# Top-k attention with two expert layers: the mask moves to ScalarE, copies out of PSUM to VectorE

## The chip, the cores and the metric

One core of a Trainium2 chip runs the whole program. The metric is the device time of one execution in microseconds; the time of a kernel is the median over its runs. The engines are TensorE (PE in the profile; PEld are its weight loads), VectorE (DVE), ScalarE (ACT), GpSimd (POOL) and SyncE (SP), which issues most of the loads. Each engine works through its own queue in program order and waits on semaphores of the others.

## The reference, cut to what matters

```python
# q, k, v: (2 batches, 8 heads, 576 tokens, 64)
scores = q @ k.T / 8
kth    = 32nd largest score of each row
scores = where(scores >= kth, scores, -1e9) - max(row)
attn   = exp(scores) / (sum(exp(scores)) + 1e-9)
x      = attn @ v                        # laid out as (1152 tokens, 512)
p      = domain_probs / (sum + 1e-9)     # (1152, 4)
x      = sum over 4 experts e of p[:, e] * (relu(x @ w1[e]) @ w2[e])   # hidden 1024
h      = max(x @ m1, x @ m2, x @ m3)     # hidden 768
out    = h @ w_out
```

Only the softmax's numerator and the ReLU outputs are touched by the change. The four last weights arrive as 64-bit floats and are turned into 32-bit floats in the kernel.

## The kernel before

The 1152 tokens are 9 tiles of 128. Four chunks of 2, 2, 2 and 3 tiles are worked on in turn, and a *pair* is one tile with two heads: 36 pairs, 8 for each of the first three chunks and 12 for the last. The tile in the middle holds tokens of both batches. A pair computes two score rows of 576 per token (`scores`, L349), copies them out of PSUM on ScalarE (L357), finds the 32 largest in seven steps of VectorE (`topk`: four MAX8, L370, and three MATCH_REPLACE8, L372), takes the exponential on ScalarE against the row's maximum (`exp`, L383), and puts those below the 32nd to zero (`mask`). The mask is one operation of VectorE with the row sum beside it (L390) for 57 of the 72 heads; for pairs 0 to 7 (second head: 0 to 6) it is two operations of GpSimd (L393, L394) and a summing copy on ScalarE (L398). Then TensorE transposes p (L408, L413), ScalarE copies the transposes out of PSUM (L411, L416), TensorE multiplies with v (L451, L454), and VectorE multiplies with the reciprocal of the sum, which went through TensorE too (L436, L438, L461).

Attention is laid out in *slots*: pair n begins at slot 8n, its second head `stag` slots later, and each step has an offset in the dictionaries `FIRST` (pairs 0 to 6), `TIGHT` (pair 7) and `LOOSE` (the rest). In a slot with `scores`, `trans`, `pv` the TensorE work is queued; what takes it out of PSUM is queued `lag` slots later.

All matmuls with weights are done as three products of high and low parts of both operands (L588 to L590), in fp32r. The weights come by SyncE's queue in tiles of 128x1024, ScalarE makes the high part (L225), GpSimd the low part (L229), from the fourth phase on VectorE every second one. A hidden activation is made in the same way: ScalarE writes the ReLU as high part (L666) and VectorE the low part from PSUM (L668); every fourth (`ON_POOL_H = 4`) is copied out first (L659) and split by ScalarE and GpSimd (L660, L661).

The products run as a generator of eight phases: the experts of chunks 0 to 3, then the last two layers of chunks 0 to 3. A planner interleaves it with the slots: `dve(n)` and `pe(n)` add planned times of VectorE (0.07 + n/960 us) and TensorE (n/2400 us), and after each slot the products go on until TensorE's planned time has caught up with VectorE's, taken times `SHARE` of the phase. The experts of a chunk begin when its x is there (`x_ready`), with the products over all but the last head pair first (`begun`). From slot 306 on, behind attention, 48 pieces of the last four weights are converted (`to_float32`, L196 to L208), stored to DRAM (L213) and loaded again as weights.

Of the kernel before, what the change touches and what calls it, by code (L numbers as in the profile page):

```python
# [10 lines left out]
F32 = mybir.dt.float32  # L11
# [3 lines left out]
AF = mybir.ActivationFunctionType  # L15
ALU = mybir.AluOpType
PSUM = bass.MemoryType.PSUM

TOPK = 32

BEGIN, READY = 4, 4
SPLIT_K, SPLIT_Q = 8, 10
ON_POOL_H = 4
ON_POOL_E = (0, 1)
H_LAG, E_LAG = 0, 0
WAITING = 3
PAUSE = 0.8
LATE = 3
ON_POOL = ((0, 1, 2, 3, 4, 5, 6, 7), (0, 1, 2, 3, 4, 5, 6))
W_FIRST, W_AHEAD = 60, 4  # L30
WIDE, W_FROM, W_STEP = 4, 306, 2

FIRST = dict(stag=2, new=1, scores=-12, trans=11, pv=17, rec=16, lag=2, sum=4)
TIGHT = dict(stag=3, new=1, scores=-7, trans=9, pv=14, rec=12, lag=1, sum=0)
LOOSE = dict(stag=4, new=1, scores=-4, trans=9, pv=16, rec=14, lag=2, sum=0)

EARLY = 7

SHARE, AHEAD = (1.0, 0.95, 1.0, 1.0), 6
AHEAD_S = 5  # L40

PHASES = [(1, 0), (1, 1), (1, 2), (1, 3), (2, 0), (2, 1), (2, 2), (2, 3)]
# [8 lines left out]
def kernel(  # L51
# [14 lines left out]
    nc = tc.nc  # L66
    B, HP, D, _, S = k.shape
    NT, DM = out.shape
    E = gates.shape[2]
    P = 128  # L70
# [3 lines left out]
    NR = S // P  # L74
    TAIL = S - NR * P
    NTILE = NT // P
    SCALE = 1.0 / float(D) ** 0.5
# [13 lines left out]
    at = ctx.enter_context(tc.tile_pool(name="at", bufs=2))  # L91
# [17 lines left out]
    def dve(n):  # L109
        clock["dve"] += 0.07 + n / 960.0  # L110

    def pe(n):
        clock["pe"] += n / 2400.0

    def bank(name):
        return pg.tile([P, 512], F32, tag="g", name=name)
# [212 lines left out]

    class Pair:  # L330
        def __init__(self, n):
            self.c, self.hp, self.t = pairs[n]
            self.s, self.w, self.m, self.nb = {}, {}, {}, {}
            self.p = self.rs = None
            self.pt = {}

            self.did = set()

            self.on_pool = [n in ON_POOL[j] for j in range(2)]

        def scores(self, j):
            srcs = [(b, i) for i, (t, b) in enumerate(SLOTS[self.c]) if t == self.t]
# [30 lines left out]

        def negate(self, j):
            m = self.m[j]
            self.nb[j] = at.tile([P, 1], F32, tag="nb%d" % j, name="nb")
            nc.scalar.activation(out=self.nb[j], in_=m[:, 0:1], func=AF.Copy, scale=-SCALE)

        def exp(self, j):
            if self.p is None:  # L380
                self.p = at.tile([P, 2, S], F32, tag="p", name="p")
                self.rs = at.tile([P, 2], F32, tag="rs", bufs=3, name="rs")
            nc.scalar.activation(out=self.p[:, j].rearrange("p (a n) -> p a n", a=2), in_=self.s[j], func=AF.Exp, bias=self.nb[j], scale=SCALE)  # L383

        def mask(self, j):
            p = self.p[:, j].rearrange("p (a n) -> p a n", a=2)
            s, kth, total = self.s[j], self.m[j][:, TOPK - 1:TOPK], self.rs[:, j:j + 1]
            if not self.on_pool[j]:
                dve(S)
                nc.vector.scalar_tensor_tensor(out=p, in0=s, scalar=kth, in1=p, op0=ALU.is_ge, op1=ALU.mult, accum_out=total)  # L390
                self.did.update([("p", j), ("sum", j)])
                return lambda: None
            nc.gpsimd.tensor_scalar(out=s, in0=s, scalar1=kth, scalar2=None, op0=ALU.is_ge)  # L393
            nc.gpsimd.tensor_tensor(out=p, in0=p, in1=s, op=ALU.mult)  # L394
            self.did.add(("p", j))

            def add():
                nc.scalar.activation(out=s, in_=p, func=AF.Copy, accum_out=total)  # L398
                self.did.add(("sum", j))
            return add  # L400

        def trans_p(self, part):
            assert {("p", j) for j in range(2) if part in (j, 2)} <= self.did
            ps = bank("psp")
            pe(260 * (NR if part < 2 else 1))
            if part < 2:
                for r in range(NR):
                    nc.tensor.transpose(ps[:, r * P:(r + 1) * P], self.p[:, part, part * TAIL + r * P:part * TAIL + (r + 1) * P], ident)  # L408
                d = at.tile([P, NR, P], F32, tag="pt%d" % part, bufs=1, name="pt")
                self.pt[part] = d  # L410
                return lambda: [nc.scalar.activation(out=d, in_=ps.rearrange("p (r n) -> p r n", r=NR), func=AF.Copy),  # L411
                                self.did.add(("pt", part))]
            nc.tensor.transpose(ps[:, 0:P], self.p.rearrange("p j s -> p (j s)")[:, NR * P:NR * P + 2 * TAIL], ident)  # L413
            d = at.tile([P, P], F32, tag="pt2", name="pt4")
            self.pt[2] = d
            return lambda: [nc.scalar.activation(out=d, in_=ps[:, 0:P], func=AF.Copy), self.did.add(("pt", 2))]  # L416

        def guard(self):
            assert {("sum", 0), ("sum", 1)} <= self.did
# [56 lines left out]
    def attention():  # L476

        NP = len(pairs)
        prs = {}
        later = {}  # L480

        def options(n):
            return FIRST if n < EARLY else TIGHT if pairs[n][0] == 0 else LOOSE

        def at_slot(s, f, *a):
            later.setdefault(s, []).append((f, a))


        first_use = {}
        for n, (c, hp, t) in enumerate(pairs):  # L490
            for b in ((0, 1) if t == MIXED else (0 if t < MIXED else 1,)):
                first_use.setdefault(("k", b, hp), n)
            first_use.setdefault(("q", c, hp), n)
        free = {"k": -99, "q": -99}
        for key, n in first_use.items():
            s0 = 8 * n
            if n == 0:
                if key[0] == "k":
                    at_slot(-60, load_first)
                    at_slot(-50, split_first)  # L500
                    free["k"] = free["q"] = -50
                    at_slot(s0, load_v, *key[1:])
                continue
            load, split = (load_k, split_k) if key[0] == "k" else (load_q, split_q)
            at = max(s0 + options(n)["scores"] - (SPLIT_K if key[0] == "k" else SPLIT_Q), free[key[0]] + 2)
            at_slot(max(at - 15, free[key[0]] + 1), load, *key[1:])
            at_slot(at, split, *key[1:])
            free[key[0]] = at
            if key[0] == "k":
                at_slot(s0, load_v, *key[1:])  # L510
        for n, (c, hp, t) in enumerate(pairs):
            s0 = 8 * n
            prs[n] = Pair(n)
            pr = prs[n]
            o = options(n)

            def two(s, f, *a, lag=o["lag"]):
                at_slot(s, lambda: at_slot(s + lag, f(*a)))
            for j in range(2):
                b0 = s0 + o["stag"] * j  # L520
                two(b0 + o["scores"], pr.scores, j)
                for i in range(7):
                    if o["new"]:
                        later.setdefault(b0 + i, []).insert(0, (pr.topk, (j, i)))
                    else:
                        at_slot(b0 + i, pr.topk, j, i)
                at_slot(b0 + 2, pr.negate, j)
                at_slot(b0 + 5, pr.exp, j)
                two(b0 + 7, pr.mask, j, lag=o["sum"] if n < EARLY else 3)
                two(b0 + o["trans"], pr.trans_p, j)  # L530
            two(s0 + o["stag"] + o["trans"], pr.trans_p, 2)
            at_slot(s0 + o["rec"] - 1, pr.guard)
            at_slot(s0 + o["rec"], pr.recip)
            at_slot(s0 + o["rec"] + 1, pr.spread)
            at_slot(s0 + o["pv"], pr.pv)
            two(s0 + o["rec"] + 2, pr.trans_r)
            end = max(o["pv"], o["rec"] + 2) + o["lag"]
            at_slot(s0 + end + 1, pr.norm)
            two(s0 + end + 2, pr.split_x)
        last = {}  # L540
        for n, p in enumerate(pairs):
            o = options(n)
            last[p[0:2]] = 8 * n + max(o["pv"], o["rec"] + 2) + 2 * o["lag"] + 2
        end = max(last.values()) + 1
        s = min(later)
        while s <= end:
            todo = later.pop(s, [])
            i = 0
            while i < len(todo):
                f, a = todo[i]  # L550
                f(*a)
                todo += later.pop(s, [])
                i += 1
            yield s, [c for c in last if last[c] + (READY if c[1] == HP - 2 else 0) == s]
            s += 1

        while narrowed[0] < WIDE * len(wide):
            clock["dve"] += PAUSE
            yield s, []
            s += 1  # L560


    lag = []
# [351 lines left out]
```

## Time and profile before

| | |
|---|---|
| median of 3 runs | 806.25 us (805.86 to 808.3) |
| profiled execution | 808.2 us, its span 806.4 us |
| busy, share of the span | PE 93%, PEld 82%, DVE 85%, ACT 61%, POOL 65% |
| granted TensorE clock, mean | 0.943 |
| chain that ended last | DVE 41%, PE 35%, DMA 8%, issue 6% |

The busy shares are means over stages with different limits, so the table says little by itself: the same TensorE runs at half its clock in the first tenth of the span and at the full clock in most of the rest.

### The profile page before, as it was taken

The page shows a single profiled execution, that of the slowest core. Times are in us where ns is not written, and L with a number is a line of the kernel's source. Part 1 is how long each engine was busy: PE and PEld are TensorE (multiplying, and loading weights), DVE is VectorE, ACT ScalarE, POOL GpSimd, SP SyncE. Part 2 cuts the span into 40 slices and gives each one's busy share as a digit, 9 for nine tenths or more (in the row PEclk, how much of TensorE's full clock was granted, in tenths as well). Part 3 has the DMA queues.
Part 4 walks back from the last instruction along what each step waited for, and adds up shares of the span by engine and source line. Part 5 has one row for each costly group of instructions (what it writes and reads, how often), then busy time and mean ns, then how long its engine had stood idle before and what let it go on. Part 6 is the DMA issues. An engine that isn't in the chain of part 4 may idle for free.

```text
span 806.4 us, 13973 instructions
## 1 busy us (share of the span) xinstructions
PE 746.3 (93%) x4942; PEld 663.2 (82%) x4942; DVE 683.8 (85%) x1242; ACT 492.7 (61%) x1027; POOL 527.2 (65%) x316
## 2 busy tenths in 40 slices
PE   3776799999999989999999999989999898999998
PEld 2454699888898879888888987879988697989996
DVE  6999989999999999999999996999999683445441
ACT  5666768677776775766777665665565444545541
POOL 2787968779888876668777685566565473555330
PEclk8556599999999999999999999999999899999999
DMA  3430245636545445253534364877777455656531
GB/s 98 117 106 13 68 131 147 190 117 173 174 137 171 135 146 151 88 169 112 161 126 146 112 188 152 270 249 250 245 251 243 157 178 167 232 165 208 178 102 40
DMA packets 50214, 126.24 MB, mean 157 GB/s; under 512 B 7904, under 2 KB 18144, under 8 KB 50144
## 3 DMA queue, kind: packets, MB, share of 16 engines
q1 hardware_dynamic: 41936, 116.69, 46.8%
q10 hardware_dynamic: 8208, 8.65, 3.1%
q8 instruction: 39, 0.64, 0.3%
q14 instruction: 31, 0.25, 0.1%
HBM read 116.67 MB, written 8.65 MB: 155 GB/s over the span
## 4 chain that ended last, share of the span: by engine, by line
DVE 41%; PE 35%; DMA 8%; issue 6%; POOL 4%; ACT 4%; SPq 2%; ACTq 0%; DVEq 0%; POOLq 0%
DVE m L370 14%; DVE work L372 13%; PE ps L588 9%; PE ps L590 9%; PE ps L589 9%; DVE p L390 6%; DMA narrow<-narrow 3%; POOL wlo L229 2%; DMA raw<-in_w_dram 2%; DVE h L668 2%; ACT whi L225 2%; SPq L246 2%; DMA kraw<-in_k_dram 1%; PE pso L590 1%; PE pso L588 1%
## 5 line engine op out<-in xcount | busy, mean ns | idle before, releaser
L229 POOL TENSOR_TENSOR wlo<-raw,whi 128x1024 fp32r<-128x1024 f32 x136 | 336.5, 2487 | 162.6 <-ACT whi L225 155.8
L225 ACT ACTIVATE whi<-raw 128x1024 fp32r<-128x1024 f32 x176 | 182.9, 1058 | 73.7 <-DMA raw<-narrow 23.8
L588 PE MATMUL ps<-xl,whi 128*128 128x256 f32 (+1 forms) x512 | 155.3, 303 | 1.7 <-DVE h L668 0.8
L370 DVE MAX8 m<-work 128x8 f32<-128x576 f32 x216 | 154.6, 742 | 0.1
L589 PE MATMUL ps<-xh,whi 128*128 128x256 f32 (+1 forms) x512 | 152.6, 298 | 0.0
L590 PE MATMUL ps<-xh,wlo 128*128 128x256 f32 (+1 forms) x512 | 152.6, 298 | 0.0
L229 DVE TENSOR_TENSOR wlo<-raw,whi 128x1024 fp32r<-128x1024 f32 x40 | 61.6, 1541 | 66.4 <-ACT whi L225 64.9
L372 DVE MATCH_REPLACE8 work<-m,work 128x576 f32<-128x576 f32 x144 | 106.4, 740 | 0.0
L588 PEld LDWEIGHTS ps<-xl,whi 128*128 128x128 f32 x512 | 99.0, 193 | 3.7 <-DVE h L668 1.3
L589 PEld LDWEIGHTS ps<-xh,whi 128*128 128x128 f32 x512 | 98.8, 193 | 0.9
L590 PEld LDWEIGHTS ps<-xh,wlo 128*128 128x128 f32 x512 | 98.7, 193 | 0.0
L590 PE MATMUL ps<-x2h,wlo 128*128 128x256 f32 (+1 forms) x288 | 85.4, 296 | 0.8 <-DVE wlo L229 0.8
L588 PE MATMUL ps<-x2l,whi 128*128 128x256 f32 (+1 forms) x288 | 85.3, 296 | 0.0
L589 PE MATMUL ps<-x2h,whi 128*128 128x256 f32 (+1 forms) x288 | 85.2, 296 | 0.0
L390 DVE SCALAR_TENSOR_TENSOR p<-s,m,p 128x576 f32<-128x576 f32 x57 | 81.0, 1422 | 0.0
L588 PE MATMUL ps<-wlo,h 128*128 128x512 f32 x192 | 77.7, 405 | 0.0
L590 PE MATMUL ps<-whi,h 128*128 128x512 f32 x192 | 75.3, 392 | 0.0
L589 PE MATMUL ps<-whi,h 128*128 128x512 f32 x192 | 75.3, 392 | 0.0
L408 PE MATMUL psp<-ident,p 128*128 128x128 f32 x288 | 50.8, 306 | 26.3 <-POOL p L394 15.4
L208 POOL TENSOR_TENSOR narrow<-narrow,raw 128x256 int32<-128x256 int32 x48 | 41.2, 858 | 44.7 <-DVE narrow L205 14.6
L349 PE MATMUL pss<-kT,ql 128*128 128x288 f32 x160 | 55.1, 358 | 13.9 <-DVE ql L293 7.6
L408 PEld LDWEIGHTS psp<-ident,p 128*128 128x128 f32 x288 | 38.3, 156 | 32.9 <-POOL p L394 18.9
(104 smaller groups left out, 1706.0 us busy)
## 6 DMA issues: line engine op xcount, KB each, us to landing
raw<-in_w_dram SPq DMA_DIRECT2D x128, 512.0 KB, 3.9
raw<-narrow SPq DMA_DIRECT2D x48, 512.0 KB, 3.8
raw<-in_m_dram SPq DMA_DIRECT2D x36, 256.0 KB, 4.4
narrow<-narrow ACTq DMA_DIRECT2D x48, 128.0 KB, 3.7
kraw<-in_k_dram SPq DMA_DIRECT2D x14, 288.0 KB, 4.5
raw<-in_mo_dram SPq DMA_DIRECT2D x12, 256.0 KB, 4.2
vt<-in_v_dram SPq DMA_DIRECT2D x8, 288.0 KB, 4.2
out_dram<-ob ACTq DMA_DIRECT2D x9, 256.0 KB, 2.0
```

The lines of the kernel that those rows point to most:

```text
L208: nc.gpsimd.tensor_tensor(out=out.bitcast(I32), in0=out.bitcast(I32), in1=last, op=ALU.add)
L225: nc.scalar.activation(out=hi, in_=raw, func=AF.Copy)
L229: on.tensor_tensor(out=lo, in0=raw, in1=hi.bitcast(F32), op=ALU.subtract)
L246: nc.sync.dma_start(out=out[half * D:(half + 1) * D], in_=src)
L349: nc.tensor.matmul(ps[:, 0:SH], lhsT=l, rhs=r, start=i == 0, stop=i == len(mm) - 1)
L370: nc.vector.max(m[:, 8 * r:8 * r + 8], src)
L372: nc.vector.match_replace(out=self.w[j], in_to_replace=m[:, 8 * r:8 * r + 8], in_values=src, imm_value=NEG)
L390: nc.vector.scalar_tensor_tensor(out=p, in0=s, scalar=kth, in1=p, op0=ALU.is_ge, op1=ALU.mult, accum_out=total)
L408: nc.tensor.transpose(ps[:, r * P:(r + 1) * P], self.p[:, part, part * TAIL + r * P:part * TAIL + (r + 1) * P], ident)
L588: nc.tensor.matmul(ps, lhsT=lh, rhs=rl, start=first, stop=False)
L589: nc.tensor.matmul(ps, lhsT=lh, rhs=rh, start=False, stop=False)
L590: nc.tensor.matmul(ps, lhsT=ll, rhs=rh, start=False, stop=last)
```

## The change

The mask goes to ScalarE for all heads. A first pass writes `prelu(kth - s)` with the slope 2^-100 on the side of the kept scores, so that those below the 32nd are positive and the kept ones are tiny and not positive; a [128, 1] operation makes the bias `kth/8 - max/8`; a second pass takes the exponential with a scale of -2^100/8, which gives the kept scores their exponential and the others zero, and sums the row. It is queued at offset 7, where the mask was (the exponential was at 5). From pair 7 on VectorE copies the transposed p out of PSUM. All low parts of ReLU outputs are made by VectorE (`ON_POOL_H = 0`). `trans`, `pv` and `rec` move one slot later in `LOOSE` and one, two and three slots earlier in `FIRST`; `SHARE` is 1 in the second phase; v is queued 8 slots later (`LATE_V`).

```diff
--- before.py
+++ after.py
@@ -19,24 +19,23 @@
 TOPK = 32
 
 BEGIN, READY = 4, 4
-SPLIT_K, SPLIT_Q = 8, 10
-ON_POOL_H = 4
+SPLIT_K, SPLIT_Q, LATE_V = 8, 10, 8
+ON_POOL_H = 0
 ON_POOL_E = (0, 1)
 H_LAG, E_LAG = 0, 0
 WAITING = 3
 PAUSE = 0.8
 LATE = 3
-ON_POOL = ((0, 1, 2, 3, 4, 5, 6, 7), (0, 1, 2, 3, 4, 5, 6))
 W_FIRST, W_AHEAD = 60, 4
 WIDE, W_FROM, W_STEP = 4, 306, 2
 
-FIRST = dict(stag=2, new=1, scores=-12, trans=11, pv=17, rec=16, lag=2, sum=4)
-TIGHT = dict(stag=3, new=1, scores=-7, trans=9, pv=14, rec=12, lag=1, sum=0)
-LOOSE = dict(stag=4, new=1, scores=-4, trans=9, pv=16, rec=14, lag=2, sum=0)
-
+FIRST = dict(stag=2, new=1, scores=-12, trans=10, pv=15, rec=13, lag=2)
+TIGHT = dict(stag=3, new=1, scores=-7, trans=9, pv=14, rec=12, lag=1)
+LOOSE = dict(stag=4, new=1, scores=-4, trans=10, pv=17, rec=15, lag=2)
 EARLY = 7
-
-SHARE, AHEAD = (1.0, 0.95, 1.0, 1.0), 6
+SMALL = 2.0 ** -100
+
+SHARE, AHEAD = (1.0, 1.0, 1.0, 1.0), 6
 AHEAD_S = 5
 
 PHASES = [(1, 0), (1, 1), (1, 2), (1, 3), (2, 0), (2, 1), (2, 2), (2, 3)]
@@ -329,14 +328,13 @@
 
     class Pair:
         def __init__(self, n):
+            self.n = n
             self.c, self.hp, self.t = pairs[n]
             self.s, self.w, self.m, self.nb = {}, {}, {}, {}
             self.p = self.rs = None
             self.pt = {}
 
             self.did = set()
-
-            self.on_pool = [n in ON_POOL[j] for j in range(2)]
 
         def scores(self, j):
             srcs = [(b, i) for i, (t, b) in enumerate(SLOTS[self.c]) if t == self.t]
@@ -373,47 +371,47 @@
 
         def negate(self, j):
             m = self.m[j]
-            self.nb[j] = at.tile([P, 1], F32, tag="nb%d" % j, name="nb")
-            nc.scalar.activation(out=self.nb[j], in_=m[:, 0:1], func=AF.Copy, scale=-SCALE)
+            self.nb[j] = at.tile([P, 2], F32, tag="nb%d" % j, name="nb")
+            nc.scalar.activation(out=self.nb[j][:, 0:1], in_=m[:, 0:1], func=AF.Copy, scale=-SCALE)
 
         def exp(self, j):
+
+
+
             if self.p is None:
                 self.p = at.tile([P, 2, S], F32, tag="p", name="p")
                 self.rs = at.tile([P, 2], F32, tag="rs", bufs=3, name="rs")
-            nc.scalar.activation(out=self.p[:, j].rearrange("p (a n) -> p a n", a=2), in_=self.s[j], func=AF.Exp, bias=self.nb[j], scale=SCALE)
-
-        def mask(self, j):
             p = self.p[:, j].rearrange("p (a n) -> p a n", a=2)
-            s, kth, total = self.s[j], self.m[j][:, TOPK - 1:TOPK], self.rs[:, j:j + 1]
-            if not self.on_pool[j]:
-                dve(S)
-                nc.vector.scalar_tensor_tensor(out=p, in0=s, scalar=kth, in1=p, op0=ALU.is_ge, op1=ALU.mult, accum_out=total)
-                self.did.update([("p", j), ("sum", j)])
-                return lambda: None
-            nc.gpsimd.tensor_scalar(out=s, in0=s, scalar1=kth, scalar2=None, op0=ALU.is_ge)
-            nc.gpsimd.tensor_tensor(out=p, in0=p, in1=s, op=ALU.mult)
-            self.did.add(("p", j))
-
-            def add():
-                nc.scalar.activation(out=s, in_=p, func=AF.Copy, accum_out=total)
-                self.did.add(("sum", j))
-            return add
+            kth, nb = self.m[j][:, TOPK - 1:TOPK], self.nb[j]
+            nc.scalar.activation(out=p, in_=self.s[j], func=AF.Prelu, bias=kth, scale=-1.0, alpha=SMALL)
+            nc.scalar.activation(out=nb[:, 1:2], in_=kth, func=AF.Identity, bias=nb[:, 0:1], scale=SCALE)
+            nc.scalar.activation(out=p, in_=p, func=AF.Exp, bias=nb[:, 1:2], scale=-SCALE / SMALL, accum_out=self.rs[:, j:j + 1])
+            self.did.update([("p", j), ("sum", j)])
+
+        def copy(self, out, ps, n):
+
+            if self.n < EARLY:
+                nc.scalar.activation(out=out, in_=ps, func=AF.Copy)
+            else:
+                dve(n)
+                nc.vector.tensor_copy(out=out, in_=ps)
 
         def trans_p(self, part):
             assert {("p", j) for j in range(2) if part in (j, 2)} <= self.did
             ps = bank("psp")
+            copy = self.copy
             pe(260 * (NR if part < 2 else 1))
             if part < 2:
                 for r in range(NR):
                     nc.tensor.transpose(ps[:, r * P:(r + 1) * P], self.p[:, part, part * TAIL + r * P:part * TAIL + (r + 1) * P], ident)
                 d = at.tile([P, NR, P], F32, tag="pt%d" % part, bufs=1, name="pt")
                 self.pt[part] = d
-                return lambda: [nc.scalar.activation(out=d, in_=ps.rearrange("p (r n) -> p r n", r=NR), func=AF.Copy),
+                return lambda: [copy(d, ps.rearrange("p (r n) -> p r n", r=NR), NR * P),
                                 self.did.add(("pt", part))]
             nc.tensor.transpose(ps[:, 0:P], self.p.rearrange("p j s -> p (j s)")[:, NR * P:NR * P + 2 * TAIL], ident)
             d = at.tile([P, P], F32, tag="pt2", name="pt4")
             self.pt[2] = d
-            return lambda: [nc.scalar.activation(out=d, in_=ps[:, 0:P], func=AF.Copy), self.did.add(("pt", 2))]
+            return lambda: [copy(d, ps[:, 0:P], P), self.did.add(("pt", 2))]
 
         def guard(self):
             assert {("sum", 0), ("sum", 1)} <= self.did
@@ -507,7 +505,7 @@
             at_slot(at, split, *key[1:])
             free[key[0]] = at
             if key[0] == "k":
-                at_slot(s0, load_v, *key[1:])
+                at_slot(s0 + LATE_V, load_v, *key[1:])
         for n, (c, hp, t) in enumerate(pairs):
             s0 = 8 * n
             prs[n] = Pair(n)
@@ -525,8 +523,7 @@
                     else:
                         at_slot(b0 + i, pr.topk, j, i)
                 at_slot(b0 + 2, pr.negate, j)
-                at_slot(b0 + 5, pr.exp, j)
-                two(b0 + 7, pr.mask, j, lag=o["sum"] if n < EARLY else 3)
+                at_slot(b0 + 7, pr.exp, j)
                 two(b0 + o["trans"], pr.trans_p, j)
             two(s0 + o["stag"] + o["trans"], pr.trans_p, 2)
             at_slot(s0 + o["rec"] - 1, pr.guard)
```

## Rows read from the trace of the kernel before

**Rows 1.** Busy times by stage: stretch, us, each engine's busy us, granted clock, DMA share, GB/s.
```profile
0.00:97.50 97.50, 62.01 (x295) 46.44 (x296) 89.03 (x194) 62.64 (x170) 70.41 (x57) 0.63 0.26 75
...
120.00:480.00 360.00, 350.21 (x2651) 311.65 (x2651) 355.30 (x721) 254.15 (x552) 280.16 (x151) 0.99 0.49 146
480.00:499.40 19.40, 16.75 (x96) 12.88 (x93) 11.41 (x19) 9.50 (x22) 9.11 (x6) 0.91 0.44 137
499.40:660.00 160.60, 154.78 (x821) 139.88 (x820) 148.06 (x208) 91.38 (x172) 94.19 (x71) 0.98 0.73 235
660.00:806.40 146.40, 140.04 (x917) 131.64 (x915) 59.93 (x63) 60.77 (x78) 58.16 (x26) 1.00 0.47 155
```

**Rows 2.** TensorE in order of time: start, us, line, operation, count, idle before, releaser.
```profile
97.50 0.41 PE L588 MATMUL ps<-xl,whi 128*128 128x256 f32 x1
...
162.77 0.47 PE L408 MATMUL psp<-ident,p 128*128 128x128 f32 x1 [2.91 <-DVE h L668]
...
489.64 0.57 PE L588 MATMUL ps<-wlo,h 128*128 128x512 f32 x1
...
499.38 0.33 PE L588 MATMUL ps<-xl,whi 128*128 128x384 f32 x1
...
637.89 0.79 PE L588 MATMUL ps<-wlo,hh 128*128 128x512 f32 x1 [3.19 <-DVE acc L697]
...
674.78 0.50 PE L588 MATMUL pso<-wlo,h 128*128 128x512 f32 x1 [1.78 <-ACT h L794]
```

**Rows 3.** Groups by line and shape. Columns: operation, count, busy us, mean ns, idle before it.
```profile
L390 DVE SCALAR_TENSOR_TENSOR p<-s,m,p 128x576 f32<-128x576 f32 x57 | 81.0, 1422 | 0.0
...
L383 ACT ACTIVATE p<-s,nb 128x576 f32<-128x576 f32 x72 | 55.8, 774 | 0.0
...
L411 ACT ACTIVATE pt<-psp 128x512 f32<-128x512 f32 x72 | 42.7, 593 | 3.1 <-PE psp L408 3.0
...
L393 POOL TENSOR_SCALAR s<-s,m 128x576 f32<-128x576 f32 x15 | 25.9, 1724 | 11.1 <-DVE m L370 5.4 <-ACT pt L416 3.4 <-ACT s L357 2.0
L668 DVE SCALAR_TENSOR_TENSOR h<-ps,h 128x512 fp32r<-128x512 f32 x36 | 24.3, 675 | 5.9 <-ACT h L666 5.9
...
L394 POOL TENSOR_TENSOR p<-p,s 128x576 f32<-128x576 f32 x15 | 21.1, 1405 | 1.3
...
L377 ACT ACTIVATE nb<-m 128x1 f32<-128x1 f32 x72 | 14.1, 198 | 12.3 <-DVE m L370 12.3
...
L461 DVE TENSOR_TENSOR xt<-psv,r 128x128 f32<-128x128 f32 x36 | 10.0, 278 | 4.4 <-ACT r L438 4.4
...
L104 ACT ACT_TABLE_LOAD x1 | 1.3, 1283 | 0.7 <-PEq L894 0.7
```

**Rows 4.** Chain of waits in order of time. Columns: start, us, what.
```profile
147.59 1.25 POOL ql L293
...
154.69 5.68 DMA raw<-in_w_dram
160.45 1.06 ACT whi L225
...
664.45 1.85 DMA narrow<-narrow
```

**Rows 5.** VectorE in order of time, two pairs' reciprocals.
```profile
81.22 0.15 DVE L427 RECIPROCAL rr<-rs 128x2 f32<-128x2 f32 x1
...
90.58 0.15 DVE L427 RECIPROCAL rr<-rs 128x2 f32<-128x2 f32 x1
```

**Rows 6.** The conversions' tile, first and last start.
```profile
L196 ACT ACTIVATE narrow<-raw x48: 412/428/453, 490.9 to 650.6; 128x256 f32<-128x256 f32 x48
```

**Rows 7.** ScalarE's waits from 120 to 480 us. Columns: total us, times, longest.
```profile
ACT nb L377 <- DVE m L370: 12.3, 12, 2.6
ACT whi L225 <- DMA raw<-in_w_dram: 12.2, 9, 4.4
...
ACT r L438 <- PE psr L436: 9.5, 11, 1.4
```

## The prediction

> **What bounds the kernel now.** I read the busy times by stage first, then TensorE's order of time at its gaps, then the chain of waits, and last the groups of instructions for prices. The stages are cut where the work changes [rows 1]. From 0 to 97.5 us only attention runs: VectorE is busy 89.0 us of 97.5, TensorE 62.0 at a granted clock of 0.63. From 97.5 to 499.4 attention and the products of the first three chunks of tokens share the chip, and TensorE and VectorE are both full: in 120 to 480 us TensorE is busy 350.2 of 360 and VectorE 355.3. From 499.4 to 660 the experts of the last chunk run while 48 pieces of weights are converted: TensorE 154.8 of 160.6, VectorE 148.1. After 660 TensorE is nearly alone, 140.0 of 146.4.
>
> So the change, which mostly unloads VectorE, has to be read from TensorE. A VectorE that has room lets the end move only by what TensorE now stands still: 9.8 us in 120 to 480, 2.7 in 480 to 499.4, 5.8 in 499.4 to 660, 6.4 after that (of which the last store is a part), and by what the lower clock costs after such stops, 0.01 of 360, 0.09 of 19.4 and 0.02 of 160.6 us: 3.6, 1.7 and 3.2 [rows 1]. That is 33 us at most. The matmuls between the gaps follow each other closely (42 of 512 columns between 489.64 and 499.38, 0.232 us each, [rows 2]) and stay as they are.
>
> **The change, part by part.** Durations are of the profiled execution: span 806.4, 808.2 with what lies around it; the median of the runs is 806.25, so I work out a difference and take it from the median.
>
> *Masks.* VectorE loses 57 masks of 1.422 us, 81.0 us [rows 3]. GpSimd loses 15 of 1.724 and 1.405, 47 us, all of it before 97.5 [rows 3]. ScalarE gains 72 first passes; the trace has none of that function, and the nearest row is its own exponential over the same tile, 0.774 us [rows 3]. Between the 0.593 of a 512-column copy below and twice the exponential above, I take 0.774; with a [128,1] operation of 0.198 [rows 3] and as much for reading the sum, 1.17 us a head, 84 us in all.
>
> *Copies out of PSUM.* 29 pairs give VectorE two copies of 512 columns and one of 128. It has none in the trace; the nearest rows read one PSUM operand too: 0.675 for 512 columns, 0.278 for 128 [rows 3]. From 0.593 (ScalarE's own copy) to 0.74 (a MAX8 of 576 columns is about that) for the large one; I take 0.675: 29 x (2 x 0.675 + 0.278) = 47.2 us. ScalarE loses about 29 x (2 x 0.593 + 0.278) = 42.5. The copy waits for TensorE's transposes; behind it on VectorE stand the MAX8 of later heads. It is queued two slots after the transposes (one for pair 7) and VectorE has room, so I price the wait at nothing; without that room each copy could hold VectorE one slot.
>
> *Low parts of ReLU outputs.* Every fourth goes from GpSimd to VectorE: 12 of 0.675 before 499.4 and 4 of two halves after it, 8.1 and at most 5.4 us. VectorE ends at 81.0 - 47.2 - 8.1 = 26 us less up to 499.4, which is 7% of that stage, and some 5 more after it. ScalarE is 254 us busy of 360 [rows 1]; its balance there is 28 pairs x (2 x 1.17 - 1.46), less 12 second copies of ReLU outputs at about the 0.6 of a 512-column copy: +17, to 271, 75%. Both have room; TensorE has not. VectorE's saving by itself is therefore worth only TensorE's gaps.
>
> *Gaps in 120 to 480.* The longest is 2.91 us at 162.77 [rows 2]. Its chain begins on GpSimd: a low part of q at 147.59 frees the buffer that SyncE's queue waits for, the weights behind it land at 160.4, ScalarE's high part follows, and the ReLU, its low part and a mask stand behind that [rows 4]. GpSimd loses 47 us of masks ahead of this place and 12 low parts along the stage, and v is queued 8 slots later, so weights come earlier. The transposes of later chunks also stand one slot later behind their mask. Against it: the exponential now stands on ScalarE behind the same weights. Of 9.8 + 3.6 us I let two thirds go: -8.8, between 0 and -13.4.
>
> *Earlier start.* In the first pairs x is ready 3 slots earlier (2 x lag + 2 behind 15 instead of 18). A pair's reciprocals are 9.36 us apart there, so a slot is 1.17 us [rows 5], and the first products, now at 97.5 [rows 2], come 3.5 us earlier: -3.5, between 0 and -3.5.
>
> *Order of TensorE.* The planner issues products against VectorE's planned time. 12 more low parts at 0.603, 29 x 1.409 for copies instead of 57 x 0.67 for masks, and the share 0.95 that becomes 1 over about a third of 360 us: 7.2 + 2.7 + 6 = 16 us more, beside the earlier start. Today 9.7 us of the third chunk's products are left when attention's last transposes are issued (489.64 to 499.38, [rows 2]). They will be spent before, and the last pair's way from mask to x has nothing under it: TensorE stands about 7 us there, clock included, instead of 2.7 + 1.7: +2.6, between 0 and +6. The last chunk's experts then start at 499.4 - 3.5 - 8.8 + 2.6 = 489.7.
>
> *The tail.* Gaps of 5.8 + 3.2 us up to 660 are mostly accumulations late on VectorE (3.19 us at 637.89, [rows 2]). GpSimd's wide low parts go, VectorE gets 5 us more: I let half of it go, -4.6, between +3 and -9. But the conversions still begin behind attention. Today the last one is stored from 664.45 and TensorE waits 1.78 us for its weights at 674.78 [rows 2, 4]. TensorE, 10 us earlier at its experts and without the 9.7 us left over, comes to that place with less under the last conversion: the 10.3 us from that store to the product, less some 3 by which ScalarE leads TensorE there today (an estimate from the planner's counts), are 7.5 us of wait instead of 1.8: +5.7, and a clock that falls after it, +1.7 as at 480 to 499.4. Between 0 and +12.
>
> Sum: -3.5 - 8.8 + 2.6 - 4.6 + 5.7 + 1.7 = -6.9; 806.25 - 6.9 = 799.4 us.
>
> **Rivals.**
> 1. *The gaps close wholly.* With 1 us left in attention, 5 at its end and 4 at the last conversion, the span is 94.0 + (401.9 - 17.8) + 6 = 484 at the experts of the last chunk, then 299 to 303: 783 to 787. For it: VectorE gets 7% of room. Against it: the gap with the longest chain is no gap of VectorE's own.
> 2. *The conversions hold the tail.* They begin about 1 us ahead of the experts, at 488.6, and last as long as today, from 490.9 [rows 6] to 664.4, 173.5 us, with VectorE 92% busy under them, or 4.4 longer with the new low parts: 662 to 666.5 plus the 142 that follow, 804 to 808.5, no change to speak of. Against it: TensorE's gaps under them are 5.8 us in all, so over most of the stage the pieces follow its pace and don't set it.
> 3. *ScalarE becomes the bound, slower.* The exponential now waits for the 32nd value, the last of seven VectorE steps, and score copies, ReLUs and high parts of weights queue behind it. Today ScalarE waits for VectorE's maxima 12 times in 120 to 480, 2.6 us at the longest [rows 7]. With 271 us of work in 360 and 12.2 + 9.5 of waits for weights and TensorE [rows 7], 67 us are free; it decides from 1.2 us of new waiting a head on. At 1.5 us, about a slot, 56 heads wait 84 us: 271 + 22 + 84 = 377 instead of 360, so 806 + 17 - 3.5 = 820. Against it: VectorE, with room, runs ahead.
> 4. *The two passes don't share a table.* The trace has one table load, 1.283 us, ahead of an Exp, and Copy, ReLU and Abs run behind it without another [rows 3]; the new function is not among them. Were it in another table, 2 loads a head would add 149 us to ScalarE in the 58 heads after 97.5: 271 + 149 = 420 against 360, and 806 + 60 = 866.
>
> The Trainium skill ("ScalarE: Activation LUTs", Table sets: the hidden batching unit) has it that functions come in named sets, that cheap ones such as relu, copy, identity and abs are in every set, and that each change to another set costs a load; it does not list this function there. By that rule the trace agrees for Copy, ReLU and Abs, and only the new function is open.
>
> **How the numbers follow.** Forecast, 795 to 803.8: 0.45. Rival 1: 0.18. Rival 2: 0.18. Rival 3: 0.13. Rival 4: 0.04. 0.02 is for a little slower in other ways. A measurement of this kernel tells some 0.3% from no change, 803.8 to 808.7. Faster 0.63, within it 0.18, slower 0.19. The range is 783 to 812: it takes in rival 1 and rival 2, and leaves out rivals 3 and 4 and a little more, 0.19.
>
> **What would show it.** No second table load; masks gone from VectorE and GpSimd; first passes of about 0.77 us and VectorE's copies of about 0.68; first products near 94 us; TensorE idle under 6 us in 120 to 480; VectorE no longer full there, waiting for TensorE; the last chunk's experts at about 490 with an idle TensorE just ahead; a wait of 5 to 10 us where the last converted weights are first used. It is wrong if ScalarE waits over 67 us more in attention, if the first pass costs twice the exponential, or if the experts of the last chunk start no earlier than 499.

## The result and the profile after

The changed kernel takes 815.16 us (median of 5; 810.92 to 816.02) against 806.25: a ratio of 1.0091, 95% interval 1.0066 to 1.0115. The forecast was 799.4 and faster. The profiled execution has a span of 813.4 us, 7.0 more than before.

The busy times by stage, in the cuts of [rows 1], of the changed kernel:

```profile
0.00:97.50 97.50, 55.22 (x313) 42.94 (x313) 86.26 (x189) 67.19 (x185) 23.47 (x26) 0.82 0.28 76
97.50:120.00 22.50, 20.57 (x152) 18.54 (x153) 19.63 (x42) 15.70 (x38) 14.47 (x9) 1.00 0.51 148
120.00:480.00 360.00, 353.36 (x2678) 313.69 (x2678) 330.55 (x697) 270.60 (x618) 252.30 (x140) 1.00 0.51 149
480.00:499.40 19.40, 14.38 (x91) 11.50 (x90) 12.43 (x29) 8.66 (x24) 2.54 (x4) 0.82 0.36 117
499.40:660.00 160.60, 155.36 (x823) 140.38 (x822) 145.08 (x207) 86.62 (x168) 84.94 (x64) 0.97 0.72 225
660.00:813.40 153.40, 139.83 (x893) 130.72 (x891) 64.31 (x75) 62.18 (x82) 59.35 (x30) 0.97 0.46 153
```

The stretch just before 120 us in the kernel before:

```profile
97.50:120.00 22.50, 22.50 (x176) 20.68 (x176) 20.10 (x42) 14.26 (x34) 15.19 (x8) 0.93 0.47 147
```

VectorE did lose its work: 330.6 us of 360 instead of 355.3. TensorE did not use it: it stands still 6.6 us there instead of 9.8, but 1.9 instead of nothing just before, and 5.0 us at a clock of 0.82 in 480 to 499.4, instead of 2.7 at 0.91. Last comes the place where the loss is: after 660 us it is busy for the same 140 us as before, in 153.4 instead of 146.4.

The chain that ended last, in which VectorE had the larger part before, goes by TensorE in the changed kernel (shares of the span, from the page of the profile):

```profile
PE 59%; DVE 12%; DMA 8%; ACT 7%; issue 7%; POOL 5%; SPq 2%; ACTq 0%; POOLq 0%; DVEq 0%
```

The groups that the change made, in the columns of [rows 3]: the first pass (L386), its [128,1] operation (L387), the exponential and the reading of its sum (L388), VectorE's copies (L397), and the table load:

```profile
L386 ACT ACTIVATE p<-s,m 128x576 f32<-128x576 f32 x72 | 56.0, 777 | 51.8 <-DVE m L368 51.6
...
L388 ACT ACTIVATE p<-p,nb 128x576 f32<-128x576 f32 x72 | 55.9, 777 | 2.3
...
L397 DVE COPY pt<-psp 128x512 f32<-128x512 f32 x58 | 39.4, 679 | 3.4 <-PE psp L406 3.2
...
L387 ACT ACTIVATE nb<-m,nb 128x1 f32<-128x1 f32 x72 | 20.5, 285 | 0.0
...
L388 ACT ACTIVATION_READ_ACCUMULATOR p<-p,nb 128x1 f32 x72 | 13.4, 187 | 0.0
...
L397 DVE COPY pt<-psp 128x128 f32<-128x128 f32 x29 | 8.1, 281 | 0.0
...
L103 ACT ACT_TABLE_LOAD x1 | 1.3, 1283 | 0.7 <-PEq L891 0.7
```

The prices are close to the forecast (0.774, 0.675, 0.278 us; the reading of the sum costs 0.187 and the [128,1] operation 0.285, both taken as 0.198), and there is one table load. So the loss is in no price of an instruction.

TensorE in order of time, the lines that answer to [rows 2] (first product; first product of the last chunk's experts; the last layer of the first chunk, where the converted weights are first needed in full):

```profile
93.73 0.37 PE L585 MATMUL ps<-xl,whi 128*128 128x256 f32 x1
...
495.33 0.42 PE L585 MATMUL ps<-xl,whi 128*128 128x384 f32 x1
...
667.16 0.48 PE L585 MATMUL pso<-wlo,h 128*128 128x512 f32 x1
...
676.70 0.80 PE L585 MATMUL pso<-wlo,h 128*128 128x512 f32 x1 [7.91 <-POOL wlo L228]
...
680.90 0.80 PE L585 MATMUL pso<-wlo,h 128*128 128x512 f32 x1 [1.28 <-DVE wlo L228]
```

Products begin 3.8 us earlier and the last experts 4.1 us earlier (499.38 before). Then 11.1 us are lost: at 667 TensorE starts the last layer and waits. The chain that ended last shows for whom (changed kernel, columns as in [rows 4]):

```profile
672.07 0.71 POOL narrow L207
672.80 1.84 DMA narrow<-narrow
674.73 3.78 DMA raw<-narrow
678.53 1.07 ACT whi L224
679.62 1.24 DVE wlo L228
680.90 0.80 PE pso L585
```

The last conversion is stored at 672.80 instead of 664.45, 8.4 us later. Conversions begin behind attention, and attention ends later: VectorE writes the last pair's x (DVE in order of time) at 495.92, in the kernel before at 490.40. The conversions follow, 496.5 instead of 490.9 [rows 6] (x before and after, then the conversions' tile, changed kernel):

```profile
490.40 0.29 DVE L461 TENSOR_TENSOR xt<-psv,r 128x128 f32<-128x128 f32 x1 [4.43 <-ACT r L438]
```
```profile
495.92 0.29 DVE L459 TENSOR_TENSOR xt<-psv,r 128x128 f32<-128x128 f32 x1 [1.92 <-ACT r L436]
```
```profile
L195 ACT ACTIVATE narrow<-raw x48: 412/435/447, 496.5 to 665.6; 128x256 f32<-128x256 f32 x48
```

So 5.6 of the 8.4 us are a later start. The other 2.8 are longer conversions, 176.3 us from the first start to the last store instead of 173.5.

What the last x waited for at the very end is not TensorE's products. These are spent at 482.66. Then TensorE stands still for VectorE's copy of the transposed p, which is queued on VectorE behind top-k steps of the last heads (TensorE in order of time, changed kernel):

```profile
488.50 1.97 PE L449 MATMUL psv<-pt,vt 128*64 128x128 f32 x14 [4.76 <-DVE pt L397]
```

### The profile page after: what moved, and what is told of

The parts are those of the page before. It is cut to its first block, busy times and chain, and to the rows that moved or that the text cites. A ratio compares the mean times of both kernels' runs of the same rounds, so it can differ in the third digit from the quotient of the medians.

```text
span 813.4 us, 13936 instructions
## 1 busy us (share of the span) xinstructions
PE 738.7 (91%) x4942; PEld 657.8 (81%) x4942; DVE 658.3 (81%) x1235; ACT 511.0 (63%) x1110; POOL 437.1 (54%) x270
## 4 chain that ended last, share of the span: by engine, by line
PE 59%; DVE 12%; DMA 8%; ACT 7%; issue 7%; POOL 5%; SPq 2%; ACTq 0%; POOLq 0%; DVEq 0%
PE ps L585 15%; PE ps L587 15%; PE ps L586 15%; DMA raw<-in_w_dram 4%; DVE work L370 3%; POOL wlo L228 3%; DVE m L368 3%; PE pss L347 3%; PE psv L449 2%; PE psp L406 2%; SPq L245 2%; PE pso L585 2%; DMA kraw<-in_k_dram 1%; PE pso L587 1%; PE pso L586 1%
## 5 line engine op out<-in xcount | busy, mean ns | idle before, releaser
L228 POOL TENSOR_TENSOR wlo<-raw,whi 128x1024 fp32r<-128x1024 f32 x136 | 326.6, 2415 | 189.5 <-ACT whi L224 169.1
L224 ACT ACTIVATE whi<-raw 128x1024 fp32r<-128x1024 f32 x176 | 182.6, 1053 | 80.0 <-DMA raw<-narrow 23.6
L228 DVE TENSOR_TENSOR wlo<-raw,whi 128x1024 fp32r<-128x1024 f32 x40 | 68.0, 1700 | 73.8 <-ACT whi L224 73.1
L386 ACT ACTIVATE p<-s,m 128x576 f32<-128x576 f32 x72 | 56.0, 777 | 51.8 <-DVE m L368 51.6
L449 PE MATMUL psv<-pt,vt 128*64 128x128 f32 (+1 forms) x640 | 49.2, 294 | 27.3 <-ACT pt L394 20.6
L449 PEld LDWEIGHTS psv<-pt,vt 128*64 128x64 f32 x640 | 37.9, 151 | 37.7 <-ACT pt L394 23.3
L347 PE MATMUL pss<-kT,ql 128*128 128x288 f32 x160 | 52.1, 339 | 13.7 <-DVE ql L292 7.5
```

Of the source, the lines that this page charges most:

```text
L224: nc.scalar.activation(out=hi, in_=raw, func=AF.Copy)
L228: on.tensor_tensor(out=lo, in0=raw, in1=hi.bitcast(F32), op=ALU.subtract)
L347: nc.tensor.matmul(ps[:, 0:SH], lhsT=l, rhs=r, start=i == 0, stop=i == len(mm) - 1)
L386: nc.scalar.activation(out=p, in_=self.s[j], func=AF.Prelu, bias=kth, scale=-1.0, alpha=SMALL)
L449: nc.tensor.matmul(ps[j * D:(j + 1) * D, cols], lhsT=vt[b, self.hp][:, j * NR + r, :], rhs=self.pt[j][:, r, cols], start=r == 0, stop=False)
```

## The experiments

The theory from this comparison, called the *order theory* in the expectations: TensorE, not VectorE, sets attention's pace. The change makes the planner issue more products ahead of attention's last pairs. These come later for it, the conversions with them, and in the tail TensorE has nothing left to do while it waits for converted weights. Its rivals: the *engine theory*, that VectorE's added low parts slow the conversions themselves, and the *ScalarE theory*, that its wait for the 32nd value holds attention up. A third rival, which no expectation names, is that VectorE's new copies hold the last pairs, as the wait of 4.76 us may suggest; call it the *copy theory*. No run takes the copies back alone, but two of the runs below bear on it. All runs were timed in five rounds against the kernel before on the same chip; times are medians, ratios are to that kernel (its medians there were 806.48 to 808.14 us), intervals are 95%. "Last x" is the start of VectorE's line that writes the last pair's x.

**Share 0.95 again in the second phase.**
```diff
-SHARE, AHEAD = (1.0, 1.0, 1.0, 1.0), 6
+SHARE, AHEAD = (1.0, 0.95, 1.0, 1.0), 6
```


> Share 0.95 again in the second phase, else as changed. Order theory (products brought forward push attention's end back, the conversions start there and the end follows them): 6 us fewer products ahead of attention's end, last x near 490 instead of 495.9, time 809 to 811. Engine theory (VectorE's added work slows the conversions themselves; order is of no matter): 814 to 816, as changed. ScalarE theory (its wait for the 32nd value holds attention): 814 to 816.

809.56 us, ratio 1.0034 (1.0014 to 1.0053). Last x at 492.1. The time is as the order theory has it, the last x 2 us later than it said. One number of the planner takes back most of the loss (ratio 1.0091 to 1.0034), with no engine's work changed.

**Share 0.94 in the second and third phase.** The same line with (1.0, 0.94, 0.94, 1.0).

> Share 0.94 in the second and third phase, else as changed: 15 to 16 us fewer products ahead of attention's end, about what the change brought forward. Order theory: last x near 481, time 800 to 804. Engine theory and ScalarE theory: 813 to 817.

798.90 us, ratio 0.9909 (0.9877 to 0.9941): faster than both kernels. Last x at 479.6; the only wait at the last layer of the first chunk is 2.11 us at 663.02, for ScalarE's h and not for weights. VectorE makes the copies here as in the changed kernel, yet the wait for them at attention's end is 0.63 us instead of 4.76:

```profile
477.46 1.09 PE L449 MATMUL psv<-pt,vt 128*64 128x128 f32 x14 [0.63 <-DVE pt L397]
```

**Share 0.90.** The same line with (1.0, 0.90, 0.90, 1.0).

> Share 0.90 in the second and third phase, else as changed: 25 us fewer products ahead of attention's end. Order theory: last x at 471 to 476, where VectorE begins to bind again, the products left over cover the conversions, time 793 to 800. Engine theory and ScalarE theory: 813 to 818.

812.66 us, ratio 1.0076 (1.005 to 1.0103): a miss by more than 12 us, at the edge of what the rivals had said. The last x, at 481.0, comes no earlier than with 0.94, while 26 us of products are left. In attention TensorE now has too little to do (busy 341.7 us, the first number after 360.00) and waits more for others, 6.5 us of it for VectorE's copies:

```profile
120.00:480.00 360.00, 341.65 (x2609) 300.93 (x2609) 334.41 (x714) 265.38 (x623) 238.42 (x136) 0.99 0.47 143
```

So putting off helps only until x comes no earlier; after that it is work moved to the end.

**Every fourth low part on GpSimd again.**
```diff
-ON_POOL_H = 0
+ON_POOL_H = 4
```


> Every fourth low part of a ReLU output on GpSimd again, else as changed. Order theory: 7 us less of planned VectorE time and so 8 us fewer products ahead of attention's end, last x near 488 to 490, conversions of the same length, 807 to 811. Engine theory: last x stays near 496, the conversions get 5 us shorter, 808 to 811. The two differ in where the time goes. ScalarE theory: more copies on ScalarE, 816 to 820.

807.58 us, ratio 1.0011 (0.9989 to 1.0033). Last x at 488.4, as the order theory has it. From there to the start of the last conversion's sum on GpSimd are 172.3 us (660.7 - 488.4) instead of 176.1 (672.0 - 495.9): 4 us of the gain are shorter conversions, as the engine theory has it. That the low parts cause them is not shown: with share 0.94 all low parts are on VectorE, and the conversions take 173.0 us to the last store, here 172.4.

**Without conversions, the kernel before and the changed one.** The weights of the last layers come from another tensor:
```diff
             if key[1] in "cd" and narrowed[0] < WIDE * (narrow_at[key[2:]] + 1):
-                return
+                src = w1[w_pos["load"] % 4, w_pos["load"] // 4 % 4]
...
-        while narrowed[0] < WIDE * len(wide):
+        while False:
```


> The kernel before with the 48 conversions left out: the last layers' weights are loaded from the first expert layer's instead, with as many loads. Order theory and engine theory alike: the gaps from 499 to 675 us go, 790 to 797.

> The changed kernel with the same conversions left out. Order theory (the conversions, begun at attention's later end, are what costs): the last chunk's experts start 4 us earlier than in the kernel before and nothing waits behind them, so 3 to 7 us below the kernel before without conversions. Engine theory (the low parts on VectorE slow the last experts) and ScalarE theory (attention itself is slower): equal to it or up to 7 us above.

797.87 us without them before (ratio 0.9877, 0.9856 to 0.9898; just above the expected 797) and 794.04 changed (0.9818, 0.9797 to 0.9838). The sign turns: without conversions the changed kernel is 3.8 us the faster one, by what its last experts start earlier (495.91 against 499.48), although its last x comes 6 us later (496.50 against 490.50). So the change loses only where there are conversions. The low parts on VectorE cost nothing to see here; but the conversions' own work is gone too, so the pair doesn't show what they cost beside it. Of 499.4 to 660 us TensorE is busy 159.6 in the changed kernel:

```profile
499.40:660.00 160.60, 159.56 (x891) 145.83 (x891) 67.23 (x83) 61.86 (x84) 55.68 (x23) 1.00 0.43 138
```

**Conversions begun 8 slots earlier, in the changed kernel.**
```diff
-WIDE, W_FROM, W_STEP = 4, 306, 2
+WIDE, W_FROM, W_STEP = 4, 298, 2
```


> Changed kernel with the conversions begun 8 slots earlier, at 298, under attention's last pairs, where VectorE has room. Order theory: the last conversion is stored 7 to 11 us earlier, the wait at the last layer shrinks from 14 us to under 6, 803 to 808. Engine theory: VectorE's work is the same, the conversions only press on attention's end, 812 to 818.

809.73 us, ratio 1.0022 (1.0003 to 1.0041). The direction is right, the size short of it: the last conversion is stored at 664.1, 8.7 us earlier, and the wait at the last layer is still 6.4 us.

**Products brought forward in the kernel before.**
```diff
-SHARE, AHEAD = (1.0, 0.95, 1.0, 1.0), 6
+SHARE, AHEAD = (1.0, 1.02, 1.06, 1.0), 6
```


> The kernel before with nothing but the planner's shares raised to 1.02 and 1.06 in the second and third phase: 16 us of products brought forward as the change does, masks and copies where they were. Order theory: attention's end 6 to 14 us later than 490.4, 813 to 822. Engine theory and ScalarE theory: no engine has other work, 804 to 808.

821.13 us, ratio 1.0169 (1.015 to 1.0187). Last x at 502.9. With masks and copies where they were, order alone costs more than the whole change. It also answers the copy theory: here ScalarE makes the copies, and TensorE waits for them at the same place nearly as long as in the changed kernel:

```profile
494.98 1.97 PE L451 MATMUL psv<-pt,vt 128*64 128x128 f32 x14 [4.36 <-ACT pt L411]
```

So this wait comes when no products are left beside the last pairs, whichever engine copies.

**Products put off in the kernel before.** The same line with (1.0, 0.93, 0.96, 1.0), and then with (1.0, 0.95, 0.98, 1.0).

> The kernel before with shares 0.93 and 0.96: some 7 us fewer products ahead of attention's end, masks and copies where they were. Order theory, with VectorE full in attention there: last x stays within 3 us of 490.4, the products left over become 16 to 18 us, the last experts start at 505 to 509, 806 to 813: without room on VectorE putting products off gains nothing. If the order alone were worth it, as the gain of shares 0.94 in the changed kernel may suggest: 798 to 802.

807.63 us, ratio 1.0022 (1.0002 to 1.0042). The time is as expected, the reason is not: the last x comes at 480.6, 10 us earlier, though VectorE seemed full there (353 us of 360). Its busy share was no bound. What eats the gain is that 23.6 us of products are left and the last experts start at 504.2.

> The kernel before with share 0.98 in the third phase, a third of what the last putting off took: how much of the gain of shares 0.94 in the changed kernel is order alone. By the runs so far the stretch from the last experts' start to the end is 307 us where 9 us of products are left at the last x, 302 where 13 are, 300 where 24 are. Order alone: 13 to 16 us left, the last experts at 500 to 502, 802 to 805. If the moved work was needed too, it stays above the 798.9 of the changed kernel with shares 0.94 by 3 us or more; if order was all, it comes down to 797 to 801.

805.38 us, ratio 0.9962 (0.9944 to 0.9979), last x at 489.6 and 10.7 us of products left, fewer than expected. The better of the two orders tried is worth some 3 us to the kernel before; the changed kernel with share 0.94 is 7 us below it.

**The mask alone on ScalarE.** The kernel before with the two passes of the change; copies stay on ScalarE, slots and shares too, and the planner is charged with `dve(S)` where VectorE masked:
```diff
-                at_slot(b0 + 5, pr.exp, j)
-                two(b0 + 7, pr.mask, j, lag=o["sum"] if n < EARLY else 3)
+                at_slot(b0 + 7, pr.exp, j)
```


> The kernel before with the mask alone on ScalarE in two passes; copies stay on ScalarE, the planner charges VectorE the same, so TensorE's order is that of the kernel before instruction by instruction. Order theory: products left at attention's end as before, VectorE has 85 us of room, last x 2 to 10 us earlier, 797 to 804. ScalarE theory (some 320 of 360 us busy with its waits on the 32nd value): last x later than 490.4, 810 to 820.

806.38 us, ratio 0.9996 (0.9979 to 1.0014): no difference, and neither forecast holds. From 120 to 480 us (columns of [rows 1]):

```profile
120.00:480.00 360.00, 349.59 (x2641) 311.13 (x2639) 288.63 (x615) 303.78 (x707) 260.27 (x149) 0.99 0.48 144
```

VectorE is at 288.6 instead of 355.3 and ScalarE at 303.8 instead of 254.2, and TensorE at 349.6 instead of 350.2. 67 us less on an engine that looked 99% full change nothing. Nor do 50 us more on ScalarE, though TensorE's waits are now all for it: 10.3 us in all, against 9.5 before. What TensorE waited for is only named differently, and the chain that ended last goes by TensorE for 56% of the span and by VectorE for 14%. That a gain by VectorE and a loss by ScalarE cancel within those 10 us is not excluded. Before, from 120 to 480 us, the three largest:

```profile
PE psp L408 <- DVE h L668: 5.3, 2, 2.9
PE psv L451 <- ACT pt L411: 1.7, 3, 1.0
PE psp L408 <- DVE p L390: 1.0, 2, 0.6
```

and with the mask alone moved:

```profile
PE psv L442 <- ACT pt L402: 7.4, 10, 1.8
PE psp L399 <- ACT r L429: 2.9, 1, 2.9
```

**Low parts on GpSimd and share 0.97.** The changed kernel with `ON_POOL_H = 4` and (1.0, 0.97, 0.97, 1.0).

> Changed kernel with every fourth low part on GpSimd and shares 0.97 in the second and third phase, which by planned times leaves as many products behind attention as shares 0.94 with the low parts on VectorE. Order theory: last x at 478 to 483, 796 to 802, as there. Engine theory: up to 5 us below it, as VectorE has less to do under the conversions.

800.62 us, ratio 0.9925 (0.9902 to 0.9948), last x at 482.8: as fast as share 0.94 within the intervals. At these shares it matters little which engine makes these low parts; how many products the planner puts ahead of attention's end does.

All profiled executions in one table, by the products left (from the last x to the last chunk's experts). A profiled execution lies up to 3.2 us off its kernel's median.

| run | last x | experts of the last chunk | left | from there to the end |
|---|---|---|---|---|
| changed | 495.9 | 495.3 | -0.6 | 318.1 |
| before, brought forward | 502.9 | 502.3 | -0.6 | 316.6 |
| changed, low parts on GpSimd | 488.4 | 487.8 | -0.6 | 314.7 |
| changed, conversions early | 494.1 | 493.5 | -0.6 | 311.4 |
| changed, 0.95 | 492.1 | 494.4 | 2.3 | 316.4 |
| changed, GpSimd and 0.97 | 482.8 | 491.0 | 8.3 | 307.8 |
| before | 490.4 | 499.4 | 9.0 | 307.0 |
| before, mask alone | 489.1 | 498.1 | 9.0 | 307.4 |
| before, 0.98 | 489.6 | 500.4 | 10.7 | 304.8 |
| changed, 0.94 | 479.6 | 492.6 | 13.0 | 301.8 |
| before, 0.93 and 0.96 | 480.6 | 504.2 | 23.6 | 300.1 |
| changed, 0.90 | 481.0 | 507.0 | 26.0 | 302.3 |
| changed, no conversions | 496.5 | 495.9 | -0.6 | 297.5 |
| before, no conversions | 490.5 | 499.5 | 9.0 | 296.6 |

With the conversions in, and begun at slot 306, the stretch to the end falls from 318 to 301 us as the products left grow from nothing to 13, and hardly after that. Without conversions it is 297 either way. In all twelve executions with conversions these take 171 to 177 us from the first start to the last store, whether they begin at 480 or at 505: their end follows attention's end. The span is the sum of the last experts' start and this stretch, and one is paid for with the other.

## Why the prediction was wrong

None of the three signs of being wrong that the prediction named was there, and yet the kernel came out slower.

*What bounds the kernel* was right for attention, and the experiment with the mask alone bears it out: TensorE is the bound, and VectorE's saving is worth at most TensorE's gaps.

*The prices* were right to about 1%, but for the [128,1] operation and the reading of the sum. *The earlier start* was right: -3.8 for -3.5.

*Gaps in 120 to 480* (-8.8) were over-sized. Idle time and clock came from 9.8 + 3.6 to 6.6 + 1.8 (the granted clock is 0.91 from 240 to 260 us), -5.0. From 97.5 to 120 there are 1.9 us of idle time where there were none, and a clock of 1.00 where it was 0.93, 1.6 us: -4.7 in all. I took the waits for VectorE to be VectorE's fault. With VectorE unloaded other waits stand in their place, as with the mask alone.

*Order of TensorE* (+2.6) had the right mechanism: products spent, TensorE idle ahead of the last experts. It measured 5.0 us idle and 19.4 x 0.18 = 3.5 us of clock, 8.5 instead of 2.7 + 1.7: +4.1. The 5.0 us are the wait for VectorE's copies, which the prediction priced at nothing because VectorE has room; with no products left, the copy stands behind the last heads' top-k. But I priced the order for TensorE alone. That the same products (16 us by planned times; 9.6 us fewer are left at the last x) stand *ahead of the last pairs' work* and so push x back has no term in the sum. The conversions' start was put at 488.6 (in the second rival) and came at 496.5. With the earlier start of 3.8, these terms give -4.4 at the last experts, where -4.1 was measured and -9.7 forecast.

*The tail* is the step that failed: forecast -4.6 + 5.7 + 1.7 = +2.8, measured 318.1 - 307.0 = +11.1. Its sum leaves the last store at 664.45; it came at 672.80. After 660 us TensorE stands still 13.6 us instead of 6.4, and from 676.7 to 683.6, after the longest wait, its granted clock is 0.50, another 3.5 us. The waits at the last converted weights were foreseen (5 to 10 us; 7.9 and 1.3 came), but as something that an earlier TensorE runs into, not as conversions that begin 5.6 us later and take 2.8 us longer. The wait of 1.78 us at 674.78 before is also, by its row, one for ScalarE's h and not for weights; h stood there behind VectorE's work, which stood behind the last converted weights' low part. Nearly nothing of the 4.6 us came back under the conversions: TensorE's idle time from 499.4 to 660 is 5.2 us instead of 5.8, at a clock of 0.97 instead of 0.98.

Of the rivals the second had the mechanism, that conversions hold the tail, with the wrong start for them; with the start at 496.5 its own sum (173.5 and 142 more) gives 812, near the measured span of 813.4. The third is refuted: ScalarE waits 40 us for VectorE's maxima in 120 to 480 instead of 12, and TensorE loses nothing by it. The fourth is refuted by the one table load. The Trainium skill ("ScalarE: Activation LUTs", Table sets: the hidden batching unit) does not list this function; here it runs beside Exp without another load.

Open is how the gain of share 0.94 over the best order tried in the kernel before (ratios 0.9909 and 0.9962) splits between the earlier start, the fewer stops of TensorE and the unloaded engines; no run parts them. Open too is what the copies, the later slots of `LOOSE` and the later loads of v do by themselves: every run of the changed kernel has all three.

## What to carry to other kernels

Where a planner paces one engine's program order by another's *planned* time, moving work between engines also moves the order: look for what then stands ahead of the piece that a later stage waits for, and set the shares anew before judging the change. An engine that is 99% busy is a bound only if taking work off it moves the end; here 67 us less moved nothing, while TensorE beside it was busy 350 us of 360. Work left over at the end of a stage is not waste if it covers the start of the next.

## What the runs showed of the hardware

- The ReLU with a slope costs what the exponential does, 777 ns for 128x576, and switches no table.
- A [128,1] operation of ScalarE with a bias from memory takes 285 ns, one with constants alone 198 (191 in the changed kernel). The Trainium skill ("ScalarE: Activation LUTs", What ACT_TABLE_LOAD costs) gives about 93 ns for each such operand; the traces, with 87 to 94 between the two, agree.
- VectorE copies 512 columns out of PSUM in 679 ns and 128 in 281, ScalarE 512 in 593 ([rows 3]).
- VectorE's mask of 128x576 in the kernel before took from 800 to 2897 ns, with a median of 1227. It took 2.26 us at 483.27, while GpSimd made a low part of weights, and 0.80 us at 494.74 in the run with products brought forward, while GpSimd stood still. So the 81.0 us of masks are no fixed price: what a mask takes differs with what runs beside it.
